# A Fourier mixing layer and a tanh-shrink MLP on one core: opening loads in halves, two raw weights and the last reads of the way back on other queues

## The chip, the cores and the metric

The kernel runs on one core of one Trainium2 chip. The metric is the device time of one execution in microseconds (us), as the median of several runs. Five engines with queues of their own work side by side: TensorE (PE in the profile; its weight loads are PEld), VectorE (DVE), ScalarE (ACT), GpSimd (POOL) and SyncE (SP). SP, ACT and POOL also issue transfers (DMAs) between memory and the on-chip buffers. An engine takes its instructions strictly in the order of the program; semaphores make it wait for others.

## The reference

```python
def _attn_ref(x, filt_r, filt_i):            # x: 8 x 3008 x 256, float32
    X = np.fft.rfft(x, axis=1)
    F = (filt_r + 1j * filt_i)[None, :, :]
    return np.fft.irfft(X * F, n=x.shape[1], axis=1).astype(np.float32)

def _moe_ref(x, w_in, w_out):                # x: 24064 x 256 tokens
    h = x @ w_in                             # 2048 wide
    return ((h - np.tanh(h)) @ w_out).astype(np.float32)

attn_out = _attn_ref(...)                    # then (8, 3008, 256) -> (24064, 256)
return _moe_ref(attn_out.reshape(B * S, D), w_in, w_out)
```

The two weights arrive as float64 and are turned into float32 on the chip.

## The kernel before

**The work.** The transform over 3008 = 64 x 47 positions is done as matrix products in two factors, there and back, with a filter between. Per batch the steps are: first products over the 64 (`first`), the way there over the 47 (`forth`, later `packed`), the filter, the way back (`back`, later `packed`), and last products (`last`), which give the tokens. Every group of four residues of one batch (48 groups, four units of the hidden width each, 192 units) then goes through `up` (tokens times w_in), `shrink` (h - tanh h) and `down` (times w_out). From unit 4 on, `up` and `down` use seven products in place of eight on sums of blocks of the weights; these sums live in `wu` and `wd`, tiles with seven blocks 0 to 6 of which 4, 5, 2 are filled by `sums` long after the raw weights are converted.

**Two phases.** The first 80 us or so are an opening in a pool of its own (`pro`): batch 0 is taken through the transform alone, PE, DVE and ACT handing each other pieces. The rest of the kernel is one long loop over units `U`, into which the transform of later batches and the conversion of weights are woven by hand. The schedule is manual: what the source says first stands first on each engine. Semaphores for transfers are few (eight for SP and ACT together, eight for POOL) and are used in turn, so a transfer's issue also waits until the transfer that had its semaphore eight issues earlier has landed.

**The start.** For each of three blocks c of eight residues the loop at L1177 loads `fh` (64 of 128 columns of the first matrix, 256 KB), which DVE copies into `f0` (L1193, L1194), and the block of x in `x0`: rows 0 to 63 on SP (L1186), rows 64 to 127 on POOL, the very first piece on ACT (L1189). `gate` (L1202) makes POOL wait for the third block's upper rows before it asks for the filters (`filters_of`, L1127). `warmer(15, ...)` (L1086) is 15 products whose result nobody reads; they run while the loads are under way. Then `first0(0)`, `first0(1)` and `first0(2)` (L1076) take the three blocks, 16 products each in groups of four, and ACT or DVE copies the results to `turnt`, a view of `wd` (L1079).

**The way back of the opening.** For slots g = 0 to 6, `there0`, `filtered` and `back0` or `back` run; L1150 and L483 write the pieces `e1` to `ct2[0]` in memory. `rest` (L1134) reads `ct2[0]` back as `e2` in two steps: rows of slots 0 to 4 (four reads of 25 rows), and of the last two slots (four reads of 7 rows). Between them stands `way_back()`, that is the last two writes of L483 on SP and on ACT. Then come `first1` (L1232: part of batch 1's first products, with results copied by ACT and written to `ct1[1]`), `warmer(8)`, and `last(0)` (L595, tile `pu`), which needs all of `e2`. Two more fillers (L1379, tile `pt`) cover the copies of `pu` into `ut` by ACT (L604) and DVE (L605, L606); then `up_plain` begins (L724).

**Raw weights.** `begun(tiles, job)` issues the load of one raw weight (512 KB); `converted` then needs one step of ACT (L181) and six of DVE. Jobs 5 and 6 go to halves of `ft`, 7 and 8 to halves of `a2`; `xy` holds the steps' results.

Of the kernel before, what the change touches and what calls it, by code (L numbers as in the profile page):

```python
# [9 lines left out]
F32 = mybir.dt.float32  # L10
# [7 lines left out]
BATCH, SEQ, DM = 8, 3008, 256  # L18
# [3 lines left out]
SG = 5  # L22
# [95 lines left out]
def kernel(  # L118
# [918 lines left out]
    with tc.tile_pool(name="tr", bufs=2) as tr, tc.manual_schedule():  # L1037
# [16 lines left out]
        with tc.tile_pool(name="pro", bufs=1) as pro, \  # L1054
# [122 lines left out]
            for c in range(3):  # L1177
                lo = int(c == 0)
                xt = big([128, 8, DM], F32, "x0")
                xs.append(xt)  # L1180
                fh = pro.tile([128, 8, 64], F32, tag="e1", bufs=4, name="fh")
                (ACT if c else nc.sync).dma_start(fh, f_d[:, 512 * c:512 * c + 512])
                if lo:
                    V.memset(xt[64:128, 0], 0.0)
                for k in (0, 4):
                    nc.sync.dma_start(xt[0:64, k:k + 4], dram(x.tensor, (8 * c + k) * DM,  # L1186
                                                              [[NR * DM, 64], [1, 4 * DM]]))
                    at = max(k, lo)
                    (ACT if c + k == 0 else G).dma_start(  # L1189
                        xt[64:128, at:k + 4], dram(x.tensor, (NR - 8 * c - at) * DM,  # L1190
                                                   [[NR * DM, 64], [-DM, k + 4 - at], [1, DM]]))
                r = 8 * c
                V.tensor_copy(f0[:, r:r + 8, 0:64], fh)  # L1193
                V.tensor_scalar(out=f0[:, r:r + 8, 64:128], in0=fh,  # L1194
                                scalar1=sgn, scalar2=None, op0=ALU.mult)
# [6 lines left out]
            G.tensor_copy(gate, xs[2][64:65, 0, 0:1])  # L1202
            fts = {0: filters_of(0)}

            warmer(15, filt[2][:, 0])
            first0(0)
            first0(1)
            began.append(begun(tiles0, jobs[0], queue=nc.sync))
# [18 lines left out]
            def first1(x1):  # L1227

                for r in range(0, 8, 2):
                    pf = z0("pf", [128, 2, DM])  # L1230
                    for k in range(2):
                        nc.tensor.matmul(pf[:, k], f0[:, r + k], x1[:, r + k],  # L1232
                                         start=True, stop=True)
                    if r % 4 == 0:
                        two = (tr.tile([128, 2, 2, DM], F32, tag="a1", bufs=1, name="a1") if r else
                               buffer("xy").rearrange("p (m n) c -> p m n c", m=2))
                    a1 = two[:, r // 2 % 2]
                    ACT.copy(a1, pf)
                    nc.sync.dma_start(
                        dram(ct1[1], r * DM, [[NH * DM, 128], [1, 2 * DM]]), a1)  # L1240
                    yield

            a2 = {0: across(0)}
            convert(5)
# [19 lines left out]
            for g in range(last_g + 1):  # L1264
                if g == 2:
                    x1 = load_x(big([128, 8, DM], F32, "x1"), 1, 0, 8)
                if g + 2 <= last_g:
                    a2[g + 2] = across(g + 2)
                    if g + 2 < last_g:
                        fts[g + 2] = filters_of(g + 2)  # L1270
                        if g == 1:
                            fts[last_g] = filters_of(last_g)
                    else:
                        turned_in(fts[last_g])
                if g == 3:
                    under(fts[last_g])
                    e2s[0] = load_e2(0, 0, ())
                if g < last_g:
                    there[g + 1] = there0(g + 1)
                if g == last_g - 1:  # L1280
                    ahead += [begun(tiles1, job, queue=G) for job in jobs[7:9]]
                    next(began[3])
                    way_back()
                next(there[g][0])
                if g < last_g - 2:
                    convert(3 if g < 3 else 1)
                xy = there.pop(g)[1]
                chain = filtered(g, xy, fts.pop(g), V, V if g in (0, last_g - 1, last_g) else G, pro)
                nn = next(chain)
                for _ in range(2):  # L1290
                    next(chain)
                if g in summed:
                    next(chain)
                ended.append((back, (0, g, xy, z0, (ACT, nc.sync))) if g in summed else (back0, (g, nn)))
                if g == 1:
                    next(turning)
                if g not in (0, last_g - 1):
                    way_back()
                if g == 2:
                    next(turning)  # L1300
                if g == 3:
                    ahead = [begun(tiles1, job, queue=G) for job in jobs[5:7]]
            rest(0, SG * (last_g - 1), [nc.sync])
            way_back()
            rest(SG * (last_g - 1), NA - SG * (last_g - 1), [nc.sync])
            fs = first(2, z2, [(1, c) for c in range(2, NX)])
            next(fs)
            convert(100)
            for _ in first1(x1):
                pass  # L1310
            late = weights(tiles1, jobs[5:], G, ahead, 4,
                           after={6: (0,), 8: (1,), 10: (2, 4)})
            next(late)
            warmer(8)

        with tc.tile_pool(name="dn", bufs=2) as dn, \
                tc.tile_pool(name="ps", bufs=1, space=bass.MemoryType.PSUM) as ps:
# [210 lines left out]
```

## Time and profile before

| what | us |
|---|---|
| median of 3 runs (lowest, highest) | 2541.26 (2539.32, 2542.22) |
| the profiled execution, its own time | 2539.7 |
| its span, first to last instruction | 2537.8 |
| PE busy in the span | 2522.2 |
| DVE, ACT, POOL busy | 1934.3, 1694.0, 1532.4 |
| mean granted clock of PE | 0.998 |

The time is some 2 us more than the span: what lies before the first and after the last instruction. PE is busy for 99% of the span, and the chain of work that ended last consists of PE for 97%, so a change in another engine's work counts only where PE stands still, runs products that nobody needs, or runs at a lower clock. In the profile's views "idle before" is the time an engine stood still ahead of an instruction, with who ended it; SPq, ACTq and POOLq are the queues that issue transfers, shown when they issue, not when the data land. Names are the program's tiles without numbers at their ends: `e` is `e1` or `e2`, `a` is `a1` or `a2`, `ct` is `ct1` or `ct2`, `x` is `x0`, `x1` or, at L724, a result bank.

### The profile page before, as it was taken

To read this page: it belongs to the slowest core of one execution; us is meant where nothing else is said; L and a number is where in the kernel's file an instruction comes from. 1 tells how busy PE (TensorE), PEld (TensorE's weight loads), DVE (VectorE), ACT (ScalarE), POOL (GpSimd) and SP (SyncE) were. 2 spreads that over 40 slices of the span, in tenths; PEclk is the share of its full clock that TensorE was granted. 3 is DMA by queue.
4 is the path that set the end of the run, shared out by engine and by line. 5 is a ranking of instruction groups with operands and counts; after the bars stand their busy time and mean duration, and the time that the engine had idled before them with its cause. 6 is when DMAs were issued, how large, how long until landed. Compare 5 with 4: busy or idle time off the path is not lost.

```text
span 2537.8 us, 44568 instructions
## 1 busy us (share of the span) xinstructions
PE 2522.2 (99%) x17068; PEld 2173.2 (86%) x17068; DVE 1934.3 (76%) x2272; ACT 1694.0 (67%) x2552; POOL 1532.4 (60%) x1112
## 2 busy tenths in 40 slices
PE   9999999999999999999999999999999999999998
PEld 8678889888898888988888888888889888898887
DVE  6888877988688876888669886698866888555555
ACT  4666666667666766676667666666666666666665
POOL 4256666667566765676656665666655666455552
PEclk9999999999999999999999999999999999999999
DMA  8864223422343323342334322443123322110110
GB/s 247 260 161 106 71 50 101 111 69 52 87 104 94 80 72 86 82 111 59 82 85 108 88 53 71 97 115 84 36 72 84 92 66 53 26 31 19 25 23 19
DMA packets 333664, 211.37 MB, mean 83 GB/s; under 512 B 231645, under 2 KB 305531, under 8 KB 329793
## 3 DMA queue, kind: packets, MB, share of 16 engines
q1 hardware_dynamic: 319091, 184.93, 29.6%
q0 software_dynamic: 11120, 16.16, 2.2%
q10 hardware_dynamic: 3230, 7.34, 0.9%
q8 instruction: 136, 2.23, 0.4%
q14 instruction: 87, 0.71, 0.1%
HBM read 127.81 MB, written 83.39 MB: 83 GB/s over the span
## 4 chain that ended last, share of the span: by engine, by line
PE 97%; DMA 2%; DVE 1%; issue 0%; POOL 0%; SPq 0%; ACT 0%; POOLq 0%; DVEq 0%
PE o L826 44%; PE x L653 26%; PE z L653 13%; PE y L653 6%; PE pm L415 2%; PE pu L595 2%; PE o L888 1%; PE pm L351 1%; PE pf L308 1%; DMA filt<-in_filt_r_dram 1%; PE o L724 0%; DMA x<-in_x_dram 0%; PE x L724 0%; DMA ct<-e 0%; DMA filt_end<-filt 0%; PE z L724 0%
## 5 line engine op out<-in xcount | busy, mean ns | idle before, releaser
L826 PE MATMUL o<-t,wd 128*128 128x256 f32 (+1 forms) x3008 | 762.6, 376 | 0.0
L624 POOL TENSOR_TENSOR t<-h 128x512 f32<-128x512 f32 (+1 forms) x184 | 303.6, 1650 | 708.4 <-DVE h L776 642.1
L776 DVE TENSOR_TENSOR h<-h,y 128x1024 f32<-128x1024 f32 (+1 forms) x384 | 571.1, 1487 | 156.3 <-ACT y L772 156.3
L826 PEld LDWEIGHTS o<-t,wd 128*128 128x128 f32 x3008 | 568.8, 190 | 84.5 <-POOL o L858 15.1
L653 PE MATMUL x<-tu,wu 128*128 128x256 f32 (+1 forms) x2256 | 571.3, 376 | 0.0
L826 PE MATMUL o<-h,wd 128*128 128x256 f32 (+1 forms) x2256 | 569.9, 375 | 0.2 <-DVE h L776 0.2
L653 PEld LDWEIGHTS x<-tu,wu 128*128 128x128 f32 x2256 | 427.4, 190 | 53.8 <-issue 3.9
L826 PEld LDWEIGHTS o<-h,wd 128*128 128x128 f32 x2256 | 428.3, 190 | 50.9 <-issue 0.8
L659 ACT COPY s<-x 128x512 f32<-128x512 f32 (+1 forms) x188 | 109.3, 581 | 517.0 <-PE x L653 516.9
L769 ACT ACTIVATE y<-y 128x1024 f32<-128x1024 f32 (+1 forms) x384 | 399.5, 1040 | 12.1
L772 ACT ACTIVATE y<-y 128x1024 f32<-128x1024 f32 (+1 forms) x384 | 399.8, 1041 | 4.6
L766 ACT ACTIVATE y<-h 128x1024 f32<-128x1024 f32 (+1 forms) x384 | 400.6, 1043 | 2.5 <-DVE h L702 1.7
L627 POOL TENSOR_TENSOR t<-h,t 128x512 f32<-128x512 f32 (+1 forms) x184 | 338.3, 1839 | 0.0
L625 POOL TENSOR_TENSOR t<-h,t 128x512 f32<-128x512 f32 (+1 forms) x184 | 310.5, 1688 | 14.4
L626 POOL TENSOR_TENSOR t<-h 128x512 f32<-128x512 f32 (+1 forms) x184 | 277.0, 1506 | 0.0
L659 ACT COPY u<-x 128x512 f32<-128x512 f32 (+1 forms) x376 | 214.1, 569 | 71.8 <-PE x L653 69.1
L702 DVE COPY h<-x 128x512 f32<-128x512 f32 (+1 forms) x188 | 127.6, 679 | 129.0 <-PE x L653 128.8
L694 DVE TENSOR_TENSOR h<-z,u 128x512 f32<-128x512 f32 (+1 forms) x188 | 127.2, 677 | 87.8 <-ACT u L659 87.5
L653 PE MATMUL x<-ut,wu 128*128 128x256 f32 (+1 forms) x752 | 193.9, 380 | 0.0
L653 PE MATMUL y<-ut,wu 128*128 128x256 f32 (+1 forms) x752 | 190.1, 375 | 0.0
L653 PE MATMUL z<-ut,wu 128*128 128x256 f32 (+1 forms) x752 | 190.0, 375 | 0.0
L653 PE MATMUL z<-tu,wu 128*128 128x256 f32 (+1 forms) x752 | 190.0, 375 | 0.0
(218 smaller groups left out, 2933.8 us busy)
## 6 DMA issues: line engine op xcount, KB each, us to landing
ft<-filt SPq DMA_DIRECT2D x28, 1024.0 KB
ct<-nn SPq DMA_DIRECT2D x56, 512.0 KB
e<-ct SPq DMA_DIRECT2D x47, 512.0 KB
a<-ct SPq DMA_DIRECT2D x112, 192.0 KB
out_dram<-ot SPq DMA_DIRECT2D x1248, 16.0 KB
x_sb<-in_x_dram SPq DMA_DIRECT2D x110, 128.0 KB
ct<-a SPq DMA_DIRECT2D x60, 128.0 KB
ct<-x_sb SPq DMA_DIRECT2D x60, 128.0 KB
```

Of the source, the lines that this page charges most:

```text
L624: by.tensor_sub(t[0], b[0][1], b[0][0])
L625: by.tensor_sub(t[1], b[1][1], t[0])
L626: by.tensor_sub(t[2], b[1][1], b[0][1])
L627: by.tensor_sub(t[3], b[1][0], t[1])
L653: nc.tensor.matmul(bank[:, k], wu[:, q - 1, (2 * u + k) * 128:(2 * u + k + 1) * 128], rhs[q - 1], start=(first and k == 0), stop=True, ski ...
L659: ACT.copy(t, X)
L702: V.tensor_copy(h[:, 2, :, 0:w], X)
L766: ACT.activation(y[k], ht[k], AF.Arctan, scale=TURN)
L769: ACT.activation(y[k], y[k], AF.Tanh, scale=BEND)
L772: ACT.activation(y[k], y[k], AF.Square, scale=SCALE, accum_out=y_sums[:, 2 * U + k // 2:2 * U + k // 2 + 1])
L776: V.tensor_mul(ht[k], ht[k], y[k])
L826: nc.tensor.matmul(product(q), wd[:, q - 1, (2 * u + k) * 128: (2 * u + k + 1) * 128], rhs[q - 1][:, k], start=(u == 0 and k == 0 and q == ...
```

## The change

The loads of `fh` are cut in two halves of 64 rows: block 0 on SP and ACT, blocks 1 and 2 on ACT and POOL. The first filler has 10 products in place of 15, the second 12 in place of 8. `first1` keeps its copies in blocks 4 and 5 of `wu` (not in use yet) in place of a half of `xy` and of the tile `a1`, and writes each pair at once: two writes of 512 KB in place of four of 256 KB. The first four reads of `rest` go from SP to POOL. Raw weights 7 and 8 are no longer asked for on POOL in slot 5, but on SP after the first loads of batch 2, one ahead of `first1`'s writes and one behind them.

```diff
-                (ACT if c else nc.sync).dma_start(fh, f_d[:, 512 * c:512 * c + 512])
+                for half, queue in zip(rows, (ACT if c else nc.sync, G if c else ACT)):
+                    queue.dma_start(fh[half], f_d[half, 512 * c:512 * c + 512])
...
-            warmer(15, filt[2][:, 0])
+            warmer(10, filt[2][:, 0])
...
-                    if r % 4 == 0:
-                        two = (tr.tile([128, 2, 2, DM], F32, tag="a1", bufs=1, name="a1") if r else
-                               buffer("xy").rearrange("p (m n) c -> p m n c", m=2))
-                    a1 = two[:, r // 2 % 2]
-                    ACT.copy(a1, pf)
-                    nc.sync.dma_start(
-                        dram(ct1[1], r * DM, [[NH * DM, 128], [1, 2 * DM]]), a1)
-                    yield
+                    two = wu[:, 4 if r < 4 else 5].rearrange("p (m n c) -> p m n c", m=2, n=2)
+                    ACT.copy(two[:, r // 2 % 2], pf)
+                    if r % 4:
+                        nc.sync.dma_start(
+                            dram(ct1[1], (r - 2) * DM, [[NH * DM, 128], [1, 4 * DM]]),
+                            two.rearrange("p m n c -> p (m n c)"))
+                        yield
...
                 if g == last_g - 1:
-                    ahead += [begun(tiles1, job, queue=G) for job in jobs[7:9]]
                     next(began[3])
...
-            rest(0, SG * (last_g - 1), [nc.sync])
+            rest(0, SG * (last_g - 1), [G])
             way_back()
             rest(SG * (last_g - 1), NA - SG * (last_g - 1), [nc.sync])
             fs = first(2, z2, [(1, c) for c in range(2, NX)])
             next(fs)
             convert(100)
+            ahead.append(begun(tiles1, jobs[7]))
             for _ in first1(x1):
                 pass
+            ahead.append(begun(tiles1, jobs[8]))
...
-            warmer(8)
+            warmer(12)
```

What this does to the queues is seen in their order. First POOL at the start: `x0_..` are the upper rows of x, `fh_..` the halves of the first matrix, `gate` the wait ahead of the filters. Before:

```order
L1189 DMA x0_87<-in_x_dram 64x4x256
L1189 DMA x0_97<-in_x_dram 64x4x256 x2
L1189 DMA x0_106<-in_x_dram 64x4x256 x2
L1200 MEMSET filt0_77 5x512
L1200 MEMSET filt1_78 5x512
L1200 MEMSET filt2_79 5x512
L1202 COPY gate_121<-x0_106 1x1
```

Changed:

```order
L1190 DMA x0_87<-in_x_dram 64x4x256
L1183 DMA fh_99<-f 64x512
L1190 DMA x0_98<-in_x_dram 64x4x256 x2
L1183 DMA fh_109<-f 64x512
L1190 DMA x0_108<-in_x_dram 64x4x256 x2
L1201 MEMSET filt0_77 5x512
L1201 MEMSET filt1_78 5x512
L1201 MEMSET filt2_79 5x512
L1203 COPY gate_124<-x0_108 1x1
```

POOL has seven loads where it had five, and the third block's upper rows, for which `gate` waits, are now behind 256 KB of `fh`.

Second, SP at the end of the way back: `e1_..` are pieces that are written, `e2_..` the tile that is read back and that `last(0)` needs, `x_sb` and `f` loads for what follows, `ct1_1` the writes of `first1`, `a2_68` the raw weights 7 and 8. Before:

```order
L1150 DMA ct2_0<-e1_566 120x2x256
L1134 DMA e2_452<-ct2_0 25x1024 x4
L483 DMA ct2_0<-e1_608 48x2x128
L483 DMA ct2_0<-e1_615 48x2x128
L1134 DMA e2_452<-ct2_0 7x1024 x4
L295 DMA f_623<-f_both 128x512
L265 DMA x_sb_625<-in_x_dram 64x1024
L271 DMA x_sb_625<-in_x_dram 64x4x256
L265 DMA x_sb_628<-in_x_dram 64x1024
L271 DMA x_sb_628<-in_x_dram 64x4x256
L1239 DMA ct1_1<-xy_70 128x512 x2
L1239 DMA ct1_1<-a1_665 128x512 x2
```

Changed:

```order
L1150 DMA ct2_0<-e1_562 120x2x256
L483 DMA ct2_0<-e1_604 48x2x128
L483 DMA ct2_0<-e1_611 48x2x128
L1134 DMA e2_450<-ct2_0 7x1024 x4
L295 DMA f_619<-f_both 128x512
L265 DMA x_sb_621<-in_x_dram 64x1024
L271 DMA x_sb_621<-in_x_dram 64x4x256
L265 DMA x_sb_624<-in_x_dram 64x1024
L271 DMA x_sb_624<-in_x_dram 64x4x256
L175 DMA a2_68<-in_moe_w_out_dram 128x2x256
L1238 DMA ct1_1<-wu_61 128x1024 x2
L175 DMA a2_68<-in_moe_w_in_dram 128x2x256
```

The two writes of L483 no longer stand behind the four long reads, and the two raw weights stand behind the loads of batch 2.

Third, POOL at the same place, before:

```order
L456 TENSOR_TENSOR nn_519<-nn_519,xy_70 120x512
L175 DMA a2_68<-in_moe_w_out_dram 128x2x256
L175 DMA a2_68<-in_moe_w_in_dram 128x2x256
L175 DMA ft_69<-in_moe_w_in_dram 128x2x256
L175 DMA ft_69<-in_moe_w_out_dram 128x2x256
```

Changed:

```order
L456 TENSOR_TENSOR nn_517<-nn_517,xy_70 120x512
L1134 DMA e2_450<-ct2_0 25x1024 x4
L175 DMA ft_69<-in_moe_w_in_dram 128x2x256
L175 DMA ft_69<-in_moe_w_out_dram 128x2x256
```

The four reads stand where the two raw weights were, ahead of the raw weights 9 and 10.

## The prediction

> **What bounds the kernel now.** I read the page's first part, then all waits of PE, then PE's own timeline around the two places that the change touches.
>
> ```profile
> PE 2522.2 (99%) x17068; PEld 2173.2 (86%) x17068; DVE 1934.3 (76%) x2272; ACT 1694.0 (67%) x2552; POOL 1532.4 (60%) x1112
> ```
>
> PE is the bound by far. So the next question is where PE stands still. The waits of PE over the whole span (who waited for whom, us in total, times, longest):
>
> ```profile
> PE pu L595 <- DMA e<-ct: 2.1, 1, 2.1
> PE warm L1086 <- DVE filt L1175: 1.5, 1, 1.5
> PE pe L1146 <- POOL nn L456: 1.1, 1, 1.1
> PE pq L1099 <- ACT wd L1079: 0.9, 1, 0.9
> PE pa L428 <- DVE a L1104: 0.8, 1, 0.8
> PE pt L932 <- DVE o L858: 0.4, 1, 0.4
> PE pe L478 <- DVE xy L458: 0.4, 1, 0.4
> PE pu L595 <- issue: 0.3, 1, 0.3
> ```
>
> Two more of 0.2 us follow; all ten make 7.9 us, 0.3% of the span, and all but 0.6 us of it (L932 and one of the 0.2) lie in the opening. Nothing the change moves can take more out of PE's waits than that; what else it can win are fillers that nobody reads and time at a lower clock. The largest wait, at `last(0)`, is the one the change aims at. PE's timeline there (start, duration, instruction, idle before and its releaser):
>
> ```profile
> 65.87 1.10 PE L478 MATMUL pe<-xy,mats_sb 112*112 112x128 f32 x8 [0.37 <-DVE xy L458]
> 66.81 3.62 PE L1232 MATMUL pf<-x,f 128*128 128x256 f32 x16
> 70.26 3.62 PE L1086 MATMUL warm<-f 128*128 128x256 f32 x16
> 75.94 0.33 PE L595 MATMUL pu<-gt,e 64*64 64x64 f32 x4 [2.06 <-DMA e<-ct]
> 76.54 1.15 PE L595 MATMUL pu<-gt,e 64*64 64x64 f32 x60 [0.27 <-issue]
> ```
>
> and, behind two fillers, the first products of the long loop:
>
> ```profile
> 79.20 2.74 PE L724 MATMUL x<-ut,wu 128*128 128x448 f32 x4
> 81.77 1.67 PE L724 MATMUL z<-ut,wu 128*128 128x448 f32 x4
> 83.28 0.92 PE L724 MATMUL o<-ut,wu 128*128 128x448 f32 x2
> ```
>
> Sixteen products of 256 columns go by in 70.26 - 66.81 = 3.45 us, 0.216 us each; a filler is two of them, 0.43 us. After the gap of 2.06 us come light 64x64 products, and then the first four products of L724 take 81.77 - 79.20 = 2.57 us where the next four take 83.28 - 81.77 = 1.51 us. The table by stretches says why (length, then busy time of PE, PEld, DVE, ACT, POOL, granted clock, DMA share, GB/s):
>
> ```profile
> 78.00:81.00 3.00, 3.00 (x7) 1.83 (x6) 2.73 (x7) 0.99 (x3) 0.00 (x0) 0.50 1.03 240
> 81.00:82.00 1.00, 1.00 (x3) 0.41 (x3) 0.96 (x2) 0.00 (x0) 0.00 (x0) 0.82 1.01 356
> ```
>
> The granted clock is 0.50 for three us and 0.82 for the next: 3.0 + 0.18/0.5 = 3.4 us at half speed. So the stall at `pu` costs twice, once as a gap and once as a dip.
>
> **The change, part by part.** All terms are against the profiled execution, 2539.7 us; the median shown is 1.56 us above it, which I add at the end.
>
> *A, the start.* PE, DVE and POOL there, with the DMA share of one stretch, and the loads of x and of the second part of `mats_sb` (count, KB each, us from issue to landing):
>
> ```profile
> 1.45 9.10 PE L1086 MATMUL warm<-filt 120*128 120x256 f32 x30 [1.45 <-DVE filt L1175]
> 10.39 10.88 PE L1076 MATMUL pf<-f,x 128*128 128x128 f32 x96
> 32.06 0.59 PE L1144 MATMUL pe<-nn,mats_sb 120*120 120x256 f32 x2
> ```
>
> ```profile
> 15.14 0.48 DVE L1194 TENSOR_SCALAR f<-fh,sgn 128x512 f32<-128x512 f32 x1
> ```
>
> ```profile
> 1.29 3.46 POOL L1189 DMA_DIRECT2D x<-in_x_dram x5 [0.83 <-POOLq L1512]
> 15.26 0.40 POOL L1202 COPY gate<-x 1x1 f32<-1x1 f32 x1 [9.08 <-DMA x<-in_x_dram]
> 19.80 0.58 POOL L1211 DMA_DIRECT2D mats_sb<-mats  x1
> ```
>
> ```profile
> 4.00:8.00 4.00, 4.00 (x14) 3.29 (x14) 0.60 (x2) 0.14 (x1) 2.18 (x4) 1.00 1.04 245
> ```
>
> ```profile
> x<-in_x_dram POOLq DMA_DIRECT2D x5, 256.0 KB, 10.3
> mats_sb<-mats POOLq DMA_DIRECT2D x1, 168.8 KB, 9.7
> ```
>
> Five fillers fewer are ten products, 10 x 0.216 = 2.16 us at the pace above. But behind them stands data. The third block begins two thirds into `first0`, at 10.39 + 7.25 = 17.64, and its `f0` is ready at 15.14 + 0.48 = 15.62, its upper rows at 15.26 (the gate). If nothing of these moves, PE can win 17.64 - 15.62 = 2.0 us at most; I call it 1.9. They do move: POOL's queue now carries 256 KB more ahead of those rows. It brought five loads, 1280 KB, in the 14 us from 1.29 to 15.26, 2.8 us for each 256 KB, say 3. Then the rows come at 18.3 and PE loses 18.3 - 17.6 = 0.6 or so. The bytes in all are the same, and the DMA share is 1.04, full, so SP's and ACT's shorter queues give POOL a larger part late. Behind the gate, `mats_sb` is asked for at 19.80 and lands 9.7 later, 29.5; L1144 needs it at 32.06. Three us late, that makes 32.5, another 0.5. Bounds -1.9 and +1.1; the middle is -0.4, and I take -0.3.
>
> [...]
>
> *B, ahead of L478.* PE's 0.37 us there come from a DVE chain that began late:
>
> ```profile
> 62.87 0.69 DVE L447 TENSOR_TENSOR nn<-xy,filt_end 112x512 f32<-112x512 f32 x1 [2.27 <-DMA filt_end<-filt]
> ```
>
> ```profile
> 59.16 0.72 POOL L175 DMA_DIRECT2D a<-in_moe_w_in_dram  x1 [2.54 <-DMA ft<-in_moe_w_in_dram]
> ```
>
> The loads of raw weights 7 and 8, 1 MB, leave just these us; `filt_end` lands sooner, by less or more than 0.37 us. Bounds 0 and -0.37 (PE can win no more, it is busy before). DVE waited 2.27, six times what is needed, so -0.37.
>
> *C, pu's start.* The queues there:
>
> ```profile
> 66.61 1.57 SPq L1134 DMA_DIRECT2D e<-ct  x4
> 69.98 0.82 SPq L483 DMA_DIRECT2D ct<-e  x2
> 73.18 1.36 SPq L1134 DMA_DIRECT2D e<-ct  x4
> ```
>
> ```profile
> 66.97 0.33 ACTq L483 DMA_DIRECT2D ct<-e  x1
> 67.80 0.33 ACTq L483 DMA_DIRECT2D ct<-e  x1
> ```
>
> ```profile
> 82.72 0.72 POOL L175 DMA_DIRECT2D ft<-in_moe_w_in_dram  x1 [22.84 <-DVE xy L194]
> DMA to landing us min/median/max: 3.2/4.6/6.7
> ```
>
> SP's two writes of L483 stood behind the four long reads until 69.98, 3 us after ACT issued its own. Now SP can issue them as ACT does, at about 67.0 and 67.8. The last reads came 73.18 - 70.39 = 2.8 us after the second write, so now at 70.6 to 71.0; PE started 75.94 - 73.18 = 2.76 us after them, so those rows are there at about 73.8. POOL issues its four reads from 66.61 on, 0.72 each, the last at 68.8; the landing above is that of POOL's own writes to `ct` (L1150), and with it the reads land at 72.0, 73.4 or 75.5. PE is under cover meanwhile: 24 products from 70.26 end at 70.26 + 24 x 0.216 = 75.44, and with A and B at 74.8. So the fillers, not the data, set `pu`'s start, 0.50 us sooner than now: -0.50; the upper bound is the last landing, 75.5, against 75.94 - 0.67 = 75.27 (A and B alone): +0.2. Nothing on POOL stands behind these reads until 82.72, where it had stood still for 22.84 us.
>
> *D.* The 0.27 us inside `pu` are a second wait at that place, shown as issue; with all data there I count -0.27 (bounds 0 and -0.27).
>
> *E, the dip.* With PE busy up to `pu`, I expect no half speed: 2.57 - 1.51 = -1.06 for the four products. Bounds: 0 if it comes anyway, -1.7 (half of 3.4) if `pt` and the copies of `pu` gain too.
>
> *At nothing.* Raw weights 7 and 8 now land about 80 and 86 us. Their first users are ACT steps:
>
> ```profile
> 83.39 0.68 ACT L181 ACTIVATE xy<-ft 128x512 f32<-128x512 f32 x1 [4.40 <-DMA ct<-xy]
> ```
>
> ```profile
> 89.28 0.68 ACT L181 ACTIVATE xy<-a 128x512 f32<-128x512 f32 x1 [0.48 <-DVE xy L189]
> ```
>
> The 4.40 us wait on `xy`'s write goes, as `first1` now uses `wu`; so ACT comes some us sooner to job 7 and may wait for it instead. ACT had those 4.40 to lose without PE waiting once between 79 and 84, so the cover is PE's backlog of products; without it each us would count. The two writes of 512 KB in place of four of 256 KB carry the same bytes, read much later.
>
> Sum: -0.3 - 0.37 - 0.50 - 0.27 - 1.06 = -2.5; 2539.7 - 2.5 = 2537.2 profiled, + 1.56 = **2538.8** as a median. The low bounds give -1.9 - 0.37 - 0.50 - 0.27 - 1.7 = -4.7, 2536.5; the high ones +1.1 + 0.2 = +1.3, 2542.6.
>
> **The rivals.** *The dip comes anyway.* If the light 64x64 products of `pu`, and not the gap, bring the clock down, E is 0: 2539.8. For it: the drop starts about 78, two us behind the gap and right behind those products. Against it: it is the only drop after the start, and the only wait as long as 2 us. [...] Chance 0.13.
>
> *POOL's longer queue sets the opening.* A at its bound, +1.1: 2540.2. For it: the gate already waits 9.08 us and its rows are now the last of seven loads. Against it: the same bytes in all. Chance 0.10.
>
> *The reads on POOL land late (slower).* If they need the 10.3 us of POOL's loads at the start, they land at 68.8 + 10.3 = 79.1: `pu` starts 79.1 - 75.94 = 3.2 later, behind a gap of 4.3 us, twice that of now, for which I add as much half speed again, 1.1; less D, +4.0: 2545.3. From a landing at about 76.2 on the change is a loss. For it: all four long reads go to a queue that issues in 0.72 us what SP issues in 0.4. Against it: L1150's transfers of POOL, beside the loads of weights, needed 6.7 us at most. Chance 0.10.
>
> **How the numbers follow.** The forecast has 0.60, the rivals 0.13, 0.10 and 0.10, and 0.07 is left for what I don't see. That the halves bring nothing is 0.3 us and stays inside the forecast. What a measurement tells from no change is about 0.2%, 5.1 us: under 2536.2 is faster, over 2546.3 slower. Faster needs almost all low bounds at once: a fifth of the forecast, 0.12, and half of the unseen, 0.15. Slower needs the late reads at their worst or something unseen: 0.04 + 0.03 = 0.07. The rest, 0.78, is no change that can be told. The range from 2535.5 to 2542.6 holds the forecast with its bounds, the first two rivals, and a us below for the unseen; it leaves out the late reads and part of the unseen.
>
> **What would show it.** In the changed profile: `first0` starts near 10.39 - 2.16 = 8.2 and L1079's third copies within 2 us of now (A); `gate` at 15 to 18; no idle before L478 (B); SP's L483 at 67 and its last reads at 71, the wait of `pu` on `e<-ct` gone or under 0.5 us, `pu` near 74.8 (C); the clock 1.00 from 76 to 82 and L724's first four products in 1.5 us (E); no new wait of PE from 84 us on. I am wrong if `pu` still waits a us or more, if the dip stays, or if PE stands still between 8 and 45 us for more than the 3.0 us of now (1.1, 0.9, 0.8 and one of the 0.2).

## The result and the profile after

| kernel | median of 22 runs, us | lowest to highest | ratio to before, 95% interval |
|---|---|---|---|
| before | 2540.75 | 2539.32 to 2545.31 | 1 |
| changed | 2544.06 | 2541.51 to 2553.93 | 1.0016 (1.0010 to 1.0022) |

The change makes the kernel slower, by 0.16%, some 4 us. That is under the 0.2% which the prediction called no change, but clear of zero, on the other side of the forecast, and above its range (2542.6). The profiled execution of the changed kernel took 2542.49 us with a span of 2540.6 (before: 2539.7 and 2537.8), so it is one of the quicker ones and shows the mechanism small. Here are PE in the page's first part, and the first row and two later ones of all waits of PE:

```profile
PE 2523.2 (99%) x17066; PEld 2177.1 (86%) x17066; DVE 1933.7 (76%) x2272; ACT 1693.5 (67%) x2552; POOL 1535.6 (60%) x1116
```

```profile
PE pf L308 <- DMA x_sb<-in_x_dram: 2.5, 1, 2.5
...
PE pf L1076 <- DMA x<-in_x_dram: 0.5, 1, 0.5
PE pe L478 <- DVE xy L458: 0.5, 1, 0.5
```

The wait of `pu` on `e<-ct`, 2.1 us, is gone from the list, as forecast. In its place stands a wait that was not there before: 2.5 us at L308, the first products of batch 1 and 2 inside the long loop, for a load of `x_sb`. PE's timeline of the changed kernel at the way back:

```profile
70.14 5.34 PE L1086 MATMUL warm<-f 128*128 128x256 f32 x24
75.59 1.38 PE L595 MATMUL pu<-gt,e 64*64 64x64 f32 x64
76.90 1.12 PE L1380 MATMUL pt<-mats_sb 120*120 120x256 f32 x4
78.20 1.77 PE L724 MATMUL x<-ut,wu 128*128 128x448 f32 x4 [0.17 <-DVE ut L606]
79.81 1.67 PE L724 MATMUL z<-ut,wu 128*128 128x448 f32 x4
```

No gap ahead of `pu`, none inside it, and the first four products of L724 take 79.81 - 78.20 = 1.61 us where they took 2.57. The long loop begins 1 us sooner than before, and with the dip gone the gain grows to 2 us: the last row ahead of the new wait stands at 93.79, before at 95.75. Then, changed kernel:

```profile
93.79 1.67 PE L724 MATMUL x<-ut,wu 128*128 128x448 f32 x4
97.93 2.77 PE L308 MATMUL pf<-x_sb,f 128*128 128x256 f32 x8 [2.47 <-DMA x_sb<-in_x_dram]
100.48 2.60 PE L888 MATMUL o<-h,wd 128*128 128x448 f32 x4
```

and the same three rows of the kernel before:

```profile
95.75 1.67 PE L724 MATMUL x<-ut,wu 128*128 128x448 f32 x4
97.25 1.89 PE L308 MATMUL pf<-x_sb,f 128*128 128x256 f32 x8
98.98 1.67 PE L888 MATMUL o<-h,wd 128*128 128x448 f32 x4
```

From 1.96 us ahead PE falls to 100.48 - 98.98 = 1.5 us behind, in two rows, and the durations of these rows (2.77 for 1.89, 2.60 for 1.67) say that a dip has come back. The table by stretches shows it, and the DMA engines ahead of it (columns as in the prediction; first the changed kernel, then the one before):

```profile
84.00:88.00 4.00, 4.00 (x16) 2.69 (x15) 3.79 (x9) 2.51 (x6) 0.73 (x1) 1.00 1.05 393
88.00:92.00 4.00, 4.00 (x15) 2.55 (x14) 3.20 (x7) 3.94 (x7) 0.71 (x1) 1.00 0.98 320
98.00:102.00 4.00, 4.00 (x11) 2.73 (x12) 3.90 (x7) 0.95 (x2) 0.16 (x1) 0.62 0.76 272
```

```profile
84.00:88.00 4.00, 4.00 (x15) 2.66 (x14) 3.73 (x8) 3.14 (x7) 0.54 (x1) 1.00 0.91 351
88.00:92.00 4.00, 4.00 (x12) 2.09 (x11) 3.82 (x9) 3.27 (x5) 0.91 (x2) 1.00 0.78 201
```

Before, the DMA share fell to 0.91 and 0.78 between 84 and 92 us; changed, it is full (1.05 and 0.98). What is new in that queue is seen in SP's timeline, changed kernel, then before:

```profile
75.53 0.55 SPq L175 DMA_DIRECT2D a<-in_moe_w_out_dram  x1
...
77.15 0.70 SPq L175 DMA_DIRECT2D a<-in_moe_w_in_dram  x1
...
86.24 0.51 SPq L265 DMA_DIRECT2D x_sb<-in_x_dram  x1
86.80 0.61 SPq L271 DMA_DIRECT2D x_sb<-in_x_dram  x1
```

```profile
88.20 0.48 SPq L265 DMA_DIRECT2D x_sb<-in_x_dram  x1
```

The load for which PE waits is issued at 86.24, right after PE's first group of L308, from 84.32 to 86.21, has freed the buffer, on the queue that was given 1 MB more, the two raw weights. Before, it was issued at 88.20, and PE needed it 97.25 - 88.20 = 9.05 us later. In the changed kernel PE could have used it at 93.79 + 1.50 = 95.29, again 9.05 us after issue, and got it after 97.93 - 86.24 = 11.7.

The semaphore events in the traces tell when transfers landed. The raw weights themselves had landed at 81.91 and 86.80, near the forecast 80 and 86, but what SP had issued behind them was late: the load of `f`, the last one ahead of `x_sb` on this queue (L295, issued at 80.64), landed at 91.48, 5.2 us after `x_sb` was issued. `x_sb` landed at 97.65. Before, `f` landed 0.5 us after the issue of `x_sb`, and `x_sb` at 95.44, 1.8 us ahead of need.

The steps of ACT at L766, 384 in each kernel, can be matched one by one. They show where the shift arises:

```
L766 step of before at, us        90     103     114     143    304    1055    2518
changed kernel, shift in us    -1.93   +1.72   +2.43   +2.66  +2.65   +2.65   +2.66
```

From 143 us to the end the two executions run in step. The whole difference between them is decided in the first 143 us.

### The profile page after: what moved, and what is told of

The parts are those of the page before. It is cut to its first block, busy times and chain, and to the rows that moved or that the text cites. A ratio compares the mean times of both kernels' runs of the same rounds, so it can differ in the third digit from the quotient of the medians.

```text
span 2540.6 us, 44573 instructions
## 1 busy us (share of the span) xinstructions
PE 2523.2 (99%) x17066; PEld 2177.1 (86%) x17066; DVE 1933.7 (76%) x2272; ACT 1693.5 (67%) x2552; POOL 1535.6 (60%) x1116
## 4 chain that ended last, share of the span: by engine, by line
PE 96%; DMA 2%; DVE 1%; SPq 0%; issue 0%; POOL 0%; ACT 0%; POOLq 0%; DVEq 0%
PE o L826 44%; PE x L653 25%; PE z L653 13%; PE y L653 6%; PE pm L415 2%; PE pu L595 2%; PE o L888 1%; PE pm L351 1%; PE pf L308 1%; DMA x_sb<-in_x_dram 1%; DMA x<-in_x_dram 0%; DMA filt<-in_filt_r_dram 0%; PE o L724 0%; DMA filt<-in_filt_i_dram 0%; DVE nn L447 0%
## 5 line engine op out<-in xcount | busy, mean ns | idle before, releaser
L653 PE MATMUL x<-tu,wu 128*128 128x256 f32 (+1 forms) x2256 | 571.6, 376 | 0.0
L653 PEld LDWEIGHTS x<-tu,wu 128*128 128x128 f32 x2256 | 428.2, 190 | 53.0 <-issue 3.9
L766 ACT ACTIVATE y<-h 128x1024 f32<-128x1024 f32 (+1 forms) x384 | 400.6, 1043 | 2.5 <-DVE h L702 1.7
L653 PE MATMUL x<-ut,wu 128*128 128x256 f32 (+1 forms) x752 | 194.1, 381 | 0.0
L653 PE MATMUL y<-ut,wu 128*128 128x256 f32 (+1 forms) x752 | 190.2, 376 | 0.0
L653 PE MATMUL z<-ut,wu 128*128 128x256 f32 (+1 forms) x752 | 190.1, 375 | 0.0
L653 PE MATMUL z<-tu,wu 128*128 128x256 f32 (+1 forms) x752 | 190.1, 375 | 0.0
```

What stands on the lines that cost most here:

```text
L653: nc.tensor.matmul(bank[:, k], wu[:, q - 1, (2 * u + k) * 128:(2 * u + k + 1) * 128], rhs[q - 1], start=(first and k == 0), stop=True, ski ...
L766: ACT.activation(y[k], ht[k], AF.Arctan, scale=TURN)
```

## The experiments

The change has three parts that can be made one by one: the **start** (halves of `fh`, ten fillers), the **weights** (raw weights 7 and 8 on SP behind batch 2's loads), and the **reads** (reads on POOL, `first1` in `wu`, twelve fillers). Each kernel ran beside the kernel before on the same chip, 11 or 12 runs against 27 to 35.

### Both raw weights back in slot 5

```diff
                 if g == last_g - 1:
+                    ahead += [begun(tiles1, job, queue=G) for job in jobs[7:9]]
                     next(began[3])
...
-            ahead.append(begun(tiles1, jobs[7]))
             for _ in first1(x1):
                 pass
-            ahead.append(begun(tiles1, jobs[8]))
```

> The changed kernel, but raw weights 7 and 8 are asked for in slot 5 on POOL, as before. Theory T (transfers): the 1 MB of these two weights, now inside the stretch from 76 to 98 us where the DMA share is 1.0, makes the load of x_sb that is issued at 86.24 land at 97.7, and PE waits 2.47 us for it at L308; a dip of 3.41 us at half speed follows (1.7 us). By T the wait and the dip are gone: about 2.5 + 1.7 = 4 us less than the changed kernel, PE at the third group of L308 near 95.3, the time 1 to 2 us under the kernel before (ratio 0.9992 to 0.9996). Rival U (shape of the writes): not these loads but first1's two writes of 512 KB and the other moves make x_sb late; then the wait stays at 2 to 2.5 us, the dip too, and the ratio stays at 1.0016. Rival V (the kernel as a whole is shifted, and the wait is one of chance): wait of any size, no clear difference.

Median 2539.5 against 2541.28, ratio 0.9990 (0.9980 to 1.0000). The changed kernel has 1.0016 (1.0010 to 1.0022), so taking the weights back is worth some 6.6 us; T had expected about 4. PE's row at L308 has no wait; the load was issued at 88.88, 9.05 us before:

```profile
97.93 1.89 PE L308 MATMUL pf<-x_sb,f 128*128 128x256 f32 x8
```

Its profiled execution lost time elsewhere, shown by one row of the waits of PE and one of the table by stretches:

```profile
PE pe L1144 <- DVE nn L453: 1.7, 1, 1.7
```

```profile
64.00:68.00 4.00, 4.00 (x12) 3.06 (x11) 3.79 (x10) 0.59 (x1) 1.22 (x2) 0.57 0.44 143
```

DVE waited 5.25 us there for filter rows (`filt<-in_filt_i_dram` at L452; 3.44 in the changed kernel, which has no raw weights 7 and 8 in this stretch). PE stood still for 1.74 and then 0.57 us, and a dip followed. U falls: the writes of `first1` were those of the changed kernel, and the wait at L308 was gone.

### One of the two back

As above for job 7 alone; job 8 stays on SP.

> The changed kernel, but raw weight 7 alone goes back to slot 5 on POOL; weight 8 stays on SP behind first1's first writes. T: half of the bytes, 512 KB, leave the full stretch; at the 300 to 400 GB/s of that stretch these are 1.3 to 1.7 us, so the wait at L308 falls from 2.47 to 0.7 to 1.2 us, and the dip, which came after gaps of 2.06 and 2.47 us and not after 0.94, goes: the time lies near the kernel before (ratio 0.9995 to 1.0005). U: wait and time as in the changed kernel, 2 to 2.5 us and 1.0016.

PE's row at L308 (the load was issued at 90.56):

```profile
99.82 1.96 PE L308 MATMUL pf<-x_sb,f 128*128 128x256 f32 x8
```

PE was free at 98.11 + 1.50 = 99.61, so it waited 0.2 us: half of the bytes took away nearly all of the wait, somewhat more than T's 0.7 to 1.2. The median, 2543.21 against 2541.28, ratio 1.0002 (0.9990 to 1.0014), lies in T's range and is of little weight, since the runs fall in two groups, 2538.5 to 2542.1 and 2544.4 to 2548.4. The profiled one belongs to the upper group and shows what else can happen (start of PE's timeline, and a row by stretches):

```profile
12.70 11.56 PE L1076 MATMUL pf<-f,x 128*128 128x128 f32 x78 [4.86 <-DMA x<-in_x_dram]
```

```profile
12.00:16.00 4.00, 3.30 (x15) 3.30 (x16) 0.82 (x2) 0.80 (x1) 0.00 (x0) 0.50 1.05 279
```

Here PE waited 4.86 us in its first products for rows of x, with half speed behind it. The five fillers that the change took out would have covered some 2.2 us of that, an estimate from 10 products of 0.216 us.

### The weights alone

The kernel before with only `jobs[7:9]` moved to SP, at the places of the change.

> The kernel before, with only the two raw weights moved to SP at the places of the change. T: PE comes to the third group of L308 at 97.25 as before, and the x_sb load issued at 88.20, now with 1 MB more ahead of it or beside it (2.6 to 3.5 us of transfers), lands at 96.7 to 98.5 where it landed at 94.1; the wait of PE is 0 to 1.3 us, seldom with a dip: ratio 1.0000 to 1.0010, not faster. U: no new wait at L308, ratio 0.9995 to 1.0003. In both the stall at pu and the dip behind it stay as before.

Median 2546.42 against 2541.28, ratio 1.0021 (1.0010 to 1.0032): this part alone makes the kernel slower, and the 1.0016 of the whole change lies in its interval. PE at L308, and a row by stretches:

```profile
99.25 3.75 PE L308 MATMUL pf<-x_sb,f 128*128 128x256 f32 x8 [4.50 <-ACT xy L181]
```

```profile
100.00:104.00 4.00, 4.00 (x10) 2.84 (x9) 3.90 (x7) 1.03 (x3) 0.08 (x1) 0.50 0.71 244
```

The view names ACT, whose copies of the earlier group had ended at 97.98; what came last was `x_sb` again, issued at 85.53, 13.7 us before PE could start, and landed at 99.11. T had the cause right and the wait too small (0 to 1.3 expected): it had PE come at 97.25 as before, with a load that keeps its place in time. But the load is issued when PE's first group ends, so a PE that comes sooner brings its own deadline forward, and the 9.05 us stay: 93.08 + 1.50 - 85.53. (The 94.1 in the expectation is no landing in the trace of the kernel before, where the two halves of the load landed at 93.06 and 95.44.)

### The weights ahead of batch 2's loads

Both `begun` lines stand ahead of `fs = first(2, ...)` instead.

> The changed kernel, but both raw weights are issued on SP right behind the last reads of the way back, ahead of the loads of batch 2, so at about 72.5 and 73.1 us in place of 75.5 and 77.2. From 70 to 75 us the DMA share was 0.39, so 2 to 3 us of transfers lie free there. T: the same bytes then pass mostly before the full stretch begins, the wait at L308 falls to 0 to 1 us and the dip goes; ratio to the kernel before 0.9993 to 1.0000. U: wait as in the changed kernel, 1.0016. If the loads of batch 2, now behind 1 MB, come too late instead, PE waits at the first group of L308 (84.32) for x_sb or f.

Median 2545.55, ratio 1.0024 (1.0009 to 1.0039); no better than the changed kernel. The expectation fell, in this form:

```profile
99.94 3.64 PE L308 MATMUL pf<-x_sb,f 128*128 128x256 f32 x8 [3.77 <-DMA x_sb<-in_x_dram]
```

```profile
72.00:76.00 4.00, 4.00 (x20) 3.36 (x18) 3.79 (x8) 0.75 (x2) 0.00 (x0) 1.00 0.35 75
```

The two weights were issued at 73.84 and 74.30, 1.7 and 2.9 us sooner than in the changed kernel, and landed at 77.77 and 80.17. The free stretch was hardly used: the DMA share was 0.20 to 0.27 from 73 to 75 us and full from 75 on (0.98 from 76 to 80 us), so most of it lay ahead of the issue or in the first 1.2 us behind it. What stood behind the weights on SP kept its delay: `f` landed 8.6 us after the issue of `x_sb`, which landed at 99.69.

### The weights on POOL, behind its reads

```diff
             rest(0, SG * (last_g - 1), [G])
+            ahead += [begun(tiles1, job, queue=G) for job in jobs[7:9]]
...
-            ahead.append(begun(tiles1, jobs[7]))
...
-            ahead.append(begun(tiles1, jobs[8]))
```

> The changed kernel, but raw weights 7 and 8 go to POOL right behind its four long reads, so they are issued near 68 us, where the DMA share was 0.45 and SP's queue is not lengthened. T in its sharper form (what delays x_sb is 1 MB ahead of it in or beside SP's queue from 76 us on): these bytes have passed by 76 us, no wait or under 0.5 us at L308, no dip, ratio 0.9988 to 0.9996 like the version with both weights back in slot 5. If instead any place behind the way back is too late, the wait stays at 2 us or more. If the 1 MB delays the reads on POOL's queue or the last reads on SP, PE waits at pu.

The profiled execution did what T says: issued at 67.53 and 68.27, no wait at L308 (PE at 96.44, the load issued at 87.39), no dip, span 2537.1, the shortest of the profiled executions, with two waits at `pu` of 0.39 and 0.59 us. The median missed T's range: 2542.89, ratio 1.0007 (0.9996 to 1.0018), runs from 2537.96 to 2550.26. A single profile doesn't tell what the longer runs met; that 1 MB beside the last reads of the way back makes `pu` late is likely and not shown.

### The start alone, and the change without it

The kernel before with the first two edits of the diff; and the changed kernel with these two undone.

> The kernel before, with only the start changed: fh in halves on two queues, ten products' worth of fillers in place of fifteen. In the changed kernel this part brought 22.20 - 21.10 = 1.1 us at L1099. If it carries through (theory S+), the ratio to the kernel before is 0.9994 to 0.9998, with the stall at pu and its dip as before and no wait at L308. Rival S-: with five fillers fewer nothing covers a late landing of x; one profiled run showed PE waiting 4.86 us at L1076 and then 6.8 us at half speed (3.4 us lost). If that is common, the times spread upward by 5 to 10 us and the median is not below the kernel before (ratio 1.0000 or more).

> The changed kernel with the start of the kernel before (fh whole, fifteen fillers); weights and reads stay changed. T: the wait for x_sb at L308 stays at 1.5 to 4 us with a dip behind it, since the load is issued when PE's earlier group frees its buffer and so moves with PE: ratio 1.0010 to 1.0025. Rival E (PE simply comes too early): PE comes 1.1 us later to L308, the wait falls by 1.1 us to about 1.4, the dip goes, and the ratio is 1.0000 to 1.0005. By S- the spread of the times is smaller than that of the changed kernel (2541.5 to 2553.9).

The start alone: median 2541.09 against 2540.86, ratio 1.0000 (0.9991 to 1.0009). PE reached L1099 a us sooner and had half of it left at `pu`:

```profile
21.15 1.06 PE L1099 MATMUL pq<-one_sb,wd 128*120 128x128 f32 x8 [0.93 <-ACT wd L1079]
...
75.47 0.33 PE L595 MATMUL pu<-gt,e 64*64 64x64 f32 x4 [2.18 <-DMA e<-ct]
```

Its first gap at `pu`, 2.18 us, is followed by a dip as before. From 114 us to the end this execution is 0.32 us ahead of the kernel before. So S+ (a gain that carries through) is not shown, though the interval leaves room for its 0.9994, and S- (a common loss) is not seen: the runs spread from 2539.12 to 2544.14, no wider than before. The change without the start: median 2545.85, ratio 1.0023 (1.0012 to 1.0034). The wait stayed, though PE's opening was the old one:

```profile
97.84 3.61 PE L308 MATMUL pf<-x_sb,f 128*128 128x256 f32 x8 [2.22 <-ACT xy L181]
```

The load was issued at 86.41, 11.4 us before. Rival E was hardly put to the test: PE came to the first group of L308 at 84.49, only 0.17 us later than in the changed kernel (84.32), not the 1.1 us that E needed. What speaks against E is that the issue of the load moves with PE, and that with the weights ahead PE came 0.7 us later than in the changed kernel (85.03) and waited longer. The spread that S- wanted smaller is 2542.15 to 2552.57, about that of the changed kernel.

### The reads alone

> The kernel before, with only the way back changed: the four long reads on POOL, first1's copies in wu and its writes in pairs, twelve fillers. Weights in slot 5 on POOL and the start as before. Forecast by the prediction's terms C, D and E: 0.50 + 0.27 + 1.06 = 1.8 us less, ratio 0.9990 to 0.9996, no wait at pu, clock 1.00 from 76 to 82, no wait at L308. Rival: the reads on POOL land late or the extra fillers only replace the wait; then the ratio is 0.9998 or more.

Median 2539.2 against 2540.86, ratio 0.9994 (0.9985 to 1.0002), in the expected range, without a wait at `pu` and without a dip. Its profile also shows where an early gain ends. At 124 us PE is 1.35 us ahead of the kernel before, and then come these rows of PE, and of the stretch around them:

```profile
140.23 1.13 PE L653 MATMUL z<-ut,wu 128*128 128x256 f32 x4 [0.24 <-DVE h L694]
141.96 1.13 PE L653 MATMUL x<-ut,wu 128*128 128x256 f32 x4 [0.60 <-DVE h L702]
```

```profile
128.00:142.00 14.00, 13.16 (x48) 8.43 (x46) 13.66 (x27) 8.24 (x13) 3.50 (x4) 1.00 0.87 253
```

DVE is busy for 13.66 of these 14 us, with conversions of weights and sums (L183 to L232) among its work for the units. In the kernel before PE comes there later (141.00 at the first of these rows) and doesn't wait. At the L766 step of 143 us this execution is 0.20 us behind, and stays so to the end.

### The late load on another queue

The changed kernel, with the two transfers of that one `x_sb` load issued on ACT.

```diff
-        nc.sync.dma_start(t[0:64, 0:n, :], ...)
+        queue.dma_start(t[0:64, 0:n, :], ...)
...
-                          b, XH * c, XH), f
+                          b, XH * c, XH, ACT if also and k == 2 else nc.sync), f
```

> The changed kernel with one edit: the two transfers of the x_sb load that PE waits for at L308 (issued on SP at 86.24 and 86.80 in the changed kernel) are issued on ACT, behind its copies of the first group, near 87. Nothing else moves; the two raw weights stay on SP. PE needs the load 95.29 - 86.24 = 9.05 us after the first group has freed the buffer, in every kernel of this study. Theory Q (queue): the load is late because it stands in SP's queue behind the 1 MB of raw weights and what follows them; on ACT's queue, empty at that time, it lands in under 8 us, the wait at L308 is 0 to 0.5 us, no dip behind it, and the ratio to the kernel before is 0.9988 to 0.9998. Theory B (bytes): the 16 DMA engines are full from 76 us on, and any load issued at 87 us is late whatever its queue; the wait stays at 1.5 us or more, ratio 1.0010 or more.

```profile
96.34 1.89 PE L308 MATMUL pf<-x_sb,f 128*128 128x256 f32 x8
```

```profile
87.36 0.50 ACTq L265 DMA_DIRECT2D x_sb<-in_x_dram  x1
```

With all the bytes as in the changed kernel the wait and the dip are gone, so B falls: with the DMA engines full (a share of 1.00 from 87 to 96 us) the load landed 6.7 us after its issue, at 94.10. That the queue did it, as Q has it, is likely and not shown, for SP's backlog happened to be short: `f` landed 2.5 us after the issue of `x_sb`, as in the kernel with the reads alone, where the load was in time on SP too, with 0.6 us to spare. The time is 2543.5 against 2540.97, ratio 1.0008 (0.9999 to 1.0018). That is above Q's range, and the interval reaches from no loss to all of it. Of the rest the profile shows two short waits of PE at L653, at the place of the experiment above:

```profile
PE x L653 <- DVE h L702: 0.6, 1, 0.6
PE x L653 <- ACT u L659: 0.4, 1, 0.4
```

By the L766 steps this execution is 0.92 us ahead of the kernel before at 114 us and 0.88 us behind it from 199 us on. That the raw weights, still late, delay the conversions there is my reading and not tested.

### Eight fillers, and a version with everything

Both from the version with the weights back: `warmer(8)` in place of `warmer(12)`; and the `x_sb` load on ACT.

> The version with both raw weights back in slot 5, with eight fillers ahead of last(0) in place of twelve. The fillers end 8 x 0.216 = 1.73 us sooner. If the last reads set pu's start (they were issued at 70.99 in the changed kernel and 2.76 us lie between issue and use in the kernel before), PE waits there 0.3 to 1.5 us, too short for a dip after what was seen (none after 1.47 and 1.68 us, one after 1.70 and 2.06), and the time is 0 to 1.4 us less than with twelve fillers: ratio 0.998 to 0.9992. If the data are much later than that, the gap and the dip come back and the ratio is 0.9995 or more.

> The version with both raw weights back in slot 5 and the x_sb load on ACT: a version that should beat both kernels. By Q the load lands well ahead of need, PE has no wait at L308, and the ratio is 0.9985 to 0.9994; the gain over the version with the load on SP is at most the tail of runs in which it landed late (the load had 0.6 to 1.6 us to spare there). By B no difference to that version, 0.999.

Eight fillers: median 2539.12 against 2540.97, ratio 0.9992 (0.9983 to 1.0002). PE waits half a us at `pu`, and there is no dip:

```profile
76.38 1.59 PE L595 MATMUL pu<-gt,e 64*64 64x64 f32 x64 [0.54 <-DMA e<-ct]
```

With the load on ACT: 2541.01 against 2540.97, 0.9994 (0.9985 to 1.0003), at the end of Q's range and no gain over the version with the weights back. Its profiled execution lost time in the opening: PE stood still for 0.93 us ahead of L1099 and 0.78 us ahead of L428, and half speed followed from 23.14 to 26.55 us, 1.7 us lost. Of the nine traces with the changed start two have a dip in the first 30 us (this one and the one with one weight back), of the four with the old start none. So no version is shown to beat the kernel before clearly. The two best, 0.9990 and 0.9992, are the change with its weights taken back.

## Why the prediction was wrong

The third column is how long after the issue of `x_sb` the load of `f`, the last one ahead of it on SP, landed.

| kernel | x_sb issued | `f` landed, after that | PE starts the group | PE's wait | ratio |
|---|---|---|---|---|---|
| before | 88.20 | 0.5 | 97.25 | 0 | 1 |
| weights back | 88.88 | 0.5 | 97.93 | 0 | 0.9990 |
| reads alone | 86.85 | 2.6 | 95.90 | 0 | 0.9994 |
| start alone | 87.88 | 0.0 | 96.93 | 0 | 1.0000 |
| one weight back | 90.56 | 3.2 | 99.82 | 0.2 | 1.0002 |
| eight fillers, weights back | 87.23 | 1.0 | 96.28 | 0 | 0.9992 |
| weights back, load on ACT | 89.61 | 1.0 | 98.59 | 0 | 0.9994 |
| weights on POOL | 87.39 | 1.5 | 96.44 | 0 | 1.0007 |
| changed, load on ACT | 87.36 | 2.5 | 96.34 | 0 | 1.0008 |
| **changed** | 86.24 | 5.2 | 97.93 | 2.47 | 1.0016 |
| weights alone | 85.53 | 7.4 | 99.25 | 4.50 | 1.0021 |
| changed, start back | 86.41 | 4.3 | 97.84 | 2.22 | 1.0023 |
| weights ahead | 86.95 | 8.6 | 99.94 | 3.77 | 1.0024 |

**The step that failed** is the paragraph "At nothing". It asked when the two raw weights land and who reads them, and found cover for these readers. That much held: they landed at 81.91 and 86.80, and ACT read them at 83.45 and 87.33 without waiting for a load. It did not ask what stands behind them: 1 MB more on SP in a stretch whose DMA share it had itself quoted as 1.03, and behind it, on the same queue, a load that PE needs 9.05 us after its issue. So it put at nothing a term of 2.47 us of wait and 1.7 us of dip, and wrote "no new wait of PE from 84 us on". All four kernels with both weights on SP and the load behind them have the wait; no kernel without has more than 0.2 us of it, so chance (rival V) falls too. The wait comes with the backlog: none up to 2.6 us of it, 0.2 us at 3.2, and 2.2 us or more from 4.3 on. Whether the backlog counts because it stands in the same queue, or because the DMA engines are full, the runs do not separate. The price is the 2.2 to 4.5 us of the wait and a dip of 3.4 us at half speed, 1.7, or twice that in the kernel with the weights alone. The three parts, 1.0000 for the start, 0.9994 for the reads and 1.0021 for the weights, make 1.0015, and the change has 1.0016. Each of them is known to 0.001 only, so that they meet this closely is luck.

**A, the start.** Forecast -0.3, measured -1.1 at L1099. The gate came at 16.12 instead of 15.26, well inside the 3 us that I allowed, and the third block did not wait for it here. At L478 PE was only 0.12 us ahead; with B's +0.13 in it, -0.25 of A was left. That this is close to -0.3 is luck: the losses came at the first block's x and at L1146, not at the third block or `mats_sb`. PE's rows in the changed kernel, and the last of them in the kernel before:

```profile
8.49 0.39 PE L1076 MATMUL pf<-f,x 128*128 128x128 f32 x2
9.40 10.76 PE L1076 MATMUL pf<-f,x 128*128 128x128 f32 x94 [0.52 <-DMA x<-in_x_dram]
21.10 1.06 PE L1099 MATMUL pq<-one_sb,wd 128*120 128x128 f32 x8 [0.94 <-ACT wd L1079]
```

```profile
22.20 1.06 PE L1099 MATMUL pq<-one_sb,wd 128*120 128x128 f32 x8 [0.94 <-ACT wd L1079]
```

What I had not put in the sum is this wait: with the fillers gone, the first block's x is what PE waits for, by 0.5 us here and 4.86 in one execution. With it PE stood still for 3.5 us between 8 and 45 us, more than the 3.0 which the prediction had named as a sign of being wrong. As a time the start is worth nothing that can be told, 1.0000 (0.9991 to 1.0009).

**B** was wrong: the idle before L478 is 0.50 us, where 0.37 stood before. DVE's wait for `filt_end` is gone, but DVE now waited in a step ahead of it, for other filter rows, and from there to L458 it had no pause. Two rows of DVE, changed kernel:

```profile
59.17 0.69 DVE L452 TENSOR_TENSOR xy<-xy,filt 120x512 f32<-120x512 f32 x1 [3.44 <-DMA filt<-in_filt_i_dram]
...
62.74 0.69 DVE L447 TENSOR_TENSOR nn<-xy,filt_end 112x512 f32<-112x512 f32 x1
```

The trace of the start alone shows the same (3.37 us, and none for `filt_end`) with the raw weights in their old place, so it does not come from moving them.

**C and D** held. SP's writes and last reads, and POOL's reads:

```profile
66.85 1.20 SPq L483 DMA_DIRECT2D ct<-e  x2
70.99 1.42 SPq L1134 DMA_DIRECT2D e<-ct  x4
```

```profile
64.26 0.56 POOL L1134 DMA_DIRECT2D e<-ct  x1 [7.41 <-DMA ct<-e]
64.98 1.52 POOL L1134 DMA_DIRECT2D e<-ct  x3 [0.16 <-issue]
```

67 and 71 us were forecast for SP. The fillers ended at 70.14 + 24 x 0.216 = 75.3 and `pu` began at 75.59, with no wait for data. Of the 0.8 us to the forecast 74.8, B is 0.50, A 0.05, and 0.27 lie between that computed end and `pu`, as much as D had hoped to win. The rival of late reads on POOL is refuted.

**E** held at its place, -0.96 for the four products, and the rival "the dip comes anyway" is refuted: the same light products of `pu` run with the clock at 1.00 (in each stretch from 72 to 84 us). The dip went with the gap at `pu`, and a dip came with the new gap at L308.

**The size of the gain** was off too: 2.5 us less were forecast for the whole, and the change without its weights, where C, D and E happen, has 0.9990 (0.9980 to 1.0000), 0 to 5 us. That leaves room for 2.5 and does not show it, and the profile of the reads alone shows that part of an early gain is given back at 140 us, where PE waits 0.24 and 0.60 us for DVE. No rival of mine named either of the two places at which the time was decided after 90 us.

## What to carry to other kernels

Before moving a transfer to a later place, list what is issued behind it on its new queue until the DMA share falls again, and find the tightest deadline in that list; the moved transfer's own reader is only one of them. The load here that is issued when a buffer comes free had the same allowance in all eight kernels without a wait, 8.98 to 9.05 us, whether PE started the group at 95.90 or at 98.59. The gain of the reads alone, 1.35 us at 124 us, was gone at 143, behind a stretch in which DVE was busy for 13.66 of 14 us: follow the offset of matching instructions from the change to the end before calling it won.

## What the runs showed of the hardware

In the clock records of these traces each dip lasts 3.413 us or 6.827, and begins a whole number of steps of 3.413 us after the first full grant:

```
kernel                      full clock from, us   half speed from   between, us   steps of 3.413
before                                    6.257            77.937         71.68               21
changed                                   6.793            98.952         92.16               27
weights back                              6.217            64.243         58.03               17
weights back, load on ACT                 6.069            23.135         17.07                5
```

The other five traces with a dip give 2, 21, 27, 27 and 27 steps. Cut along the steps, the view by stretches gives (length less PE's busy time; the clock is that of the step behind):

```
kernel                      step, us           idle, us   clock next
reads alone                 63.02 to 66.44         1.47         1.00
start alone                 19.46 to 22.87         1.59         1.00
before                      74.52 to 77.94         1.69         0.50
eight fillers, weights back 64.41 to 67.82         1.71         1.00
weights back, load on ACT   19.72 to 23.14         1.71         0.50
weights back                19.87 to 23.28         1.72         1.00
start alone                 74.07 to 77.49         1.82         0.50
weights back                60.83 to 64.24         2.15         0.50
changed                     95.54 to 98.95         2.39         0.50
```

In all 13 traces, up to the last products, every step at full clock with 1.8 us idle or more is followed by half speed (seven steps) and none with 1.6 or less; of the four with 1.69 to 1.72, about half of a step, two are. So two gaps of 0.93 and 0.78 us in one step were followed by a dip, and one gap of 2.13 us that fell into two steps (1.12 and 1.01; eight fillers, at 10 us) by none. That PE's idle time in one such step decides, and not the length of a gap, is my inference from these rows, and no run was made to test it.

The runs of the kernels with the late load spread far more (2541.5 to 2553.9 in the changed kernel, 2539.3 to 2545.3 before, with single runs up to 2550.2 beside other kernels). Their profiled executions don't reach the upper end; what the longest ones met is open.
